# Splitting the opening loads of a fused attention and MLP kernel over two issuing engines, and reordering two later loads

## The chip, the cores and the metric

The kernel runs on one core of one Trainium2 chip. Five engines run their own instruction streams and meet only at semaphores: TensorE (PE, with its weight loads shown apart as PEld), VectorE (DVE), ScalarE (ACT), GpSimd (POOL) and SyncE (SP). SP does no arithmetic here; its queue issues nearly all transfers. The metric is the time of one execution in microseconds of device time. Before the change it is 271.74 us, the median of three runs (271.39 to 272.91).

## The reference

One transformer layer of 2048 tokens and 640 features. The input x is layer-normalised once, and the result feeds two branches whose sum is added to x.

- Attention is a linear attention with 32 heads of 20 features. Queries and keys are each multiplied by a small matrix `w_phi` per head; the feature map is the softmax of that and the softmax of its negative, side by side (40 features). Keys and values are summed over all tokens into a 40 x 20 matrix for each head; queries read from it, divided by a normaliser, and the result goes through `wo`.
- The MLP is a gated one: `silu(xn @ w1) * (xn @ w3)` of 1536 columns, times `w2`.

```
x = A_x
xn = _layernorm(x, axis=-1)
return x + _A_ref(xn, A_wqkv, A_w_phi, A_wo) + _B_ref(xn, B_w1, B_w3, B_w2)
```

All inputs and weights are bfloat16; sums are kept in float32.

## The kernel before

**Tiling.** The 2048 tokens are 16 tiles of 128 tokens (`x_tok`). Each is normalised in place and transposed into `xnT`, which has features on the partitions. Tiles 0 to 3 are transposed by PE and copied out of PSUM; tiles 4 to 15 by transposing transfers from SP's queue. From `xnT` come the values (`wv`), the keys and queries with `w_phi` folded into their weights (`Wkp`, `Wqp`), and the MLP in four blocks of 512 tokens by 12 column chunks of 128. One MLP unit is 10 matmuls of 512 columns, a tanh on ACT and two products on DVE. A fold multiplies a transposed weight (`wqkT`, loaded by a transposing transfer, keys and queries as two halves) by the block-diagonal form of `w_phi` (`BDc`); five folds make `Wkp` and five make `Wqp`.

**What sets the order.** Nothing is scheduled by hand at the level of instructions. A planner written in Python runs when the kernel is built. Fourteen streams (generators such as `norms`, `transposes`, `loads`, `attention`, `mlps`, `queries`) each offer their next step. The planner has an estimated cost for each instruction and a model of the transfers, so it knows for each step when it could start. It takes the one that could start first; among equals, the stream that stands earlier in the list. `attention` (rank 3) thus goes ahead of `mlps` (rank 12) when both could start as soon as PE is free. What the planner chose is fixed in the program: each engine then works through its list in order and waits on semaphores. So a step that is late on the chip holds up everything behind it on the same engine, whatever else could have run.

**Opening.** `first_loads` issues everything the first 20 us need. SP issues half of tile 0, tiles 1 and 2, half of `wv` (its 320 left columns, all five chunks of 128 rows), tile 3, the other half of `wv`, columns 0 to 511 of `w1` and `w3` (`w_s` in the profile), `phi`, the key half of `wqkT` and tiles 4 to 11. ACT issues one transfer, the other half of tile 0; the load of its activation table and a warm-up exponential follow in `consts`. `warm_up` and `idle` give PE matmuls without use before its first data. Tile 1's mean and variance are taken by ACT (`act_sum`), those of the other tiles by DVE; the power of -1/2 is on POOL. In DVE's list the mean of tile 1 (`scalar_op`) stands ahead of the normalising of tile 0, and the variance of tile 1 (in `act_rstd`) ahead of the statistics of tile 2.

**Middle.** When tile 9 has been transposed, `loads` issues, all on SP: columns 512 to 1023 of `w1` and `w3`, tiles 12 to 15, columns 1024 to 1535 of `w1` and `w3`, and the query half of `wqkT`. Then it goes on with the transposes of tiles 10 to 15. `attention` folds one chunk of the query weights behind each of tiles 9 to 13; `mlps` may use a column chunk `fc` only once `done["w"]` exceeds it, and no block of 512 tokens before its four tiles are transposed.

**Normalising.** `ln_apply` gives a tile from 4 on to DVE when DVE is free earlier than ACT by the planner's clocks, and else to ACT. The planner's costs are 0.45 us on DVE and 0.9 us on ACT.

Of the kernel before, what the change touches and what calls it, by code (L numbers as in the profile page):

```python
# [3 lines left out]
ACT = mybir.ActivationFunctionType  # L4
# [5 lines left out]
D = 640  # L10
# [4 lines left out]
DC = D // 128  # L15
# [232 lines left out]
def bass_parallel_sum__linear_kernel_hedgehog__glu_gated_swiglu__prompt_kernel(  # L248
# [16 lines left out]
    P = _Program(nc)  # L265
# [12 lines left out]
    def new(name, shape, dtype, offset=None):  # L278
        size = mybir.dt.size(dtype)
        for n in shape[1:]:  # L280
            size *= n
        return P.sbuf(name, shape, dtype, region(size) if offset is None else offset)
# [22 lines left out]
    x_tok = new("x_tok", [128, T, D], bf, RX)  # L305
# [5 lines left out]
    wv = new("wv", [128, DC, D], bf, RKV + 6400)  # L311
# [86 lines left out]
    x_t = A_x.rearrange("b (t p) d -> p (b t) d", p=128)  # L398
    out_t = out.rearrange("b (t p) d -> p (b t) d", p=128)
    wqkv_t = A_wqkv.rearrange("(c p) n -> p c n", p=128)  # L400
# [4 lines left out]
    def w13(a, b):  # L405
        P.dma("SP", w1_s[:, :, a:b], w1_t[:, :, a:b])
        P.dma("SP", w3_s[:, :, a:b], w3_t[:, :, a:b])

    def load_x(a, b):
        P.dma("SP", x_tok[:, a:b, :], x_t[:, a:b, :])  # L410

    def first_loads():
        def part_wv(a, b):
            P.dma("SP", wv[:, :, a:b], wqkv_t[:, :, 2 * D + a:2 * D + b])

        P.dma("SP", x_tok[:, 0, 0:320], x_t[:, 0, 0:320])
        P.dma("ACT", x_tok[:, 0, 320:D], x_t[:, 0, 320:D])
        load_x(1, 2)
        load_x(2, 3)
        part_wv(0, 320)  # L420
        load_x(3, 4)
        part_wv(320, D)
        w13(0, 512)
        P.dma("SP", phi_s[:], phi_t)
        P.dma("SP", wqkT[:, DC:2 * DC, :], A_wqkv[:, D:2 * D], True)
        load_x(4, 8)
        load_x(8, 12)
# [63 lines left out]

    def ln_apply(t):
        o, m, s, z = x_tok[:, t, :], mv[:, t, 0:1], rstd[:, t, 0:1], rstd[:, t, 1:2]
        if t < 4 or P.free["DVE"] < P.free["ACT"]:
            P.op("DVE", "tensor_scalar", [o], [o, m, s],
                 (o, o, m, s, ALU.add if t == 1 else ALU.subtract, ALU.mult),
                 cost=0.45)
        else:
            P.op("ACT", "activation", [o], [o, s, z], (o, o, ACT.Identity), dict(bias=z, scale=s),
                 cost=0.9)  # L500
# [225 lines left out]
    done = dict.fromkeys(("w", "ln", "t", "f", "k", "n", "kv", "v", "u", "qp", "qn", "qd", "q", "o", "h"), 0)  # L726

    def norms():
        yield lambda: (first_loads(), consts())
        yield lambda: act_sum(1, ACT.Copy, bst[:, 1, 0:1])  # L730
        yield lambda: (ln_half(0, 0), ln_half(0, 1), ln_rstd(0, 1))
        yield lambda: scalar_op(1, mv[:, 1, 0:1], bst[:, 1, 0:1], -1.0 / D, 0.0)
        yield lambda: act_sum(1, ACT.Square, mv[:, 1, 1:2], mv[:, 1, 0:1])
        yield lambda: ln_apply(0)
        done["ln"] = 1
        yield lambda: act_rstd(1)
        yield lambda: ln_half(2, 0)
        while done["t"] < 1:
            yield None
        yield lambda: ln_apply(1)  # L740
        done["ln"] = 2
        yield lambda: ln_half(2, 1)
        yield lambda: ln_rstd(2, 1)
        yield lambda: ln_half(3, 0)
        yield lambda: ln_apply(2)
        done["ln"] = 3
        yield lambda: (ln_half(3, 1), ln_rstd(3, 1))
# [48 lines left out]
    def loads():  # L796
        while done["t"] < 4:
            yield None
        for t in range(4, T):
            while done["ln"] <= t:  # L800
                yield None
            yield lambda t=t: P.dma("SP", xnT[:, :, t * 128:(t + 1) * 128], x_tok[:, t, :], True)
            done["t"] = t + 1
            if t == 9:
                yield lambda: (w13(512, 1024), load_x(12, 16))
                done["w"] = 8
                yield lambda: w13(1024, 1536)
                done["w"] = 12
                yield lambda: P.dma("SP", wqkT[:, 0:DC, :], A_wqkv[:, 0:D], True)
                done["f"] = 2  # L810

    def attention():
        def v(t):
            return lambda: v_tile(t, banks(2))

        yield warm_up
        for t in range(4):
            while done["t"] <= t:
                yield None
            k = banks(2)  # L820
            held.add(k // 2)
            for q in range(2):
                for i in range(DC):
                    yield lambda t=t, q=q, i=i, k=k: v_part(t, q, i, k)
            yield lambda t=t, k=k: v_store(t, k)
            held.clear()
        while done["f"] < 1:
            yield None
        for t in range(T):
            while done["t"] <= t:  # L830
                yield None
            yield lambda t=t: k_tile(t, banks(2))
            done["k"] = t + 1
            if t >= 4:
                yield v(t)
            if 9 <= t < 14:
                while done["f"] < 2:
                    yield None
                yield lambda dc=t - 9: fold_mm(0, dc, banks(2))
        yield lambda: P.dma("SP", wo_s[:], A_wo.rearrange("(c p) d -> p c d", p=128))  # L840
        done["v"] = 1
# [70 lines left out]
    def outs():  # L912
        for t in range(T):
            while done["o"] <= t or done["h"] <= t // 4:
# [4 lines left out]
    URGENT = {0: 4.0, 4: 4.0}  # L919
    PROMPT = (6, 8, 10, 11)  # L920
    streams = [norms(), transposes(), fold_k(), attention(), k_norms(), loads(), key_values(),
               q_toks(), q_norms(), queries(), q_transposes(), o_transposes(), mlps(), outs()]
    n = len(streams)
# [100 lines left out]
```

## Time and profile before

| | us |
|---|---|
| median of three runs | 271.74 (271.39 to 272.91) |
| the profiled execution | 271.42 |
| its span, first to last instruction | 269.7 |
| PE busy | 264.3 (98%) |
| DVE busy | 170.9 (63%) |
| ACT busy | 102.5 (38%) |
| POOL busy | 98.7 (37%) |
| granted clock of PE | 1.00 |

All instructions are issued from one helper line, so they are told apart by tile and operation. The name ahead of the arrow is the tile written, those behind it are read: `PS<-wv,xnT` is a value projection into PSUM, `PS<-xnT,w_s` an MLP matmul, `PS<-BDc,wqkT` a fold, `PS<-ident,x_tok` a transpose on PE. A trailing bracket gives the idle time of the engine before the instruction and what ended it. SPq and ACTq are issues of transfers by SP and ACT; a queue's issue time is not the transfer's. Matmuls overlap one another, so that the distance of their starts, and not the length of one, is what they cost.

### The profile page before, as it was taken

To read this page: it belongs to the slowest core of one execution; us is meant where nothing else is said; L and a number is where in the kernel's file an instruction comes from. 1 tells how busy PE (TensorE), PEld (TensorE's weight loads), DVE (VectorE), ACT (ScalarE), POOL (GpSimd) and SP (SyncE) were. 2 spreads that over 40 slices of the span, in tenths; PEclk is the share of its full clock that TensorE was granted. 3 is DMA by queue.
4 is the path that set the end of the run, shared out by engine and by line. 5 is a ranking of instruction groups with operands and counts; after the bars stand their busy time and mean duration, and the time that the engine had idled before them with its cause. 6 is when DMAs were issued, how large, how long until landed. Compare 5 with 4: busy or idle time off the path is not lost.

```text
span 269.7 us, 4850 instructions
## 1 busy us (share of the span) xinstructions
PE 264.3 (98%) x1978; PEld 161.4 (60%) x1978; DVE 170.9 (63%) x304; ACT 102.5 (38%) x197; POOL 98.7 (37%) x127
## 2 busy tenths in 40 slices
PE   7899999999999999999999999999999999999996
PEld 4556677567855545445445445455677777777774
DVE  4449899999727977778877779877553331212112
ACT  5547989798364343433243433344300000000000
POOL 4315849899974432244421344412440100000000
PEclk9999999999999999999999999999999999999999
DMA  7980589951093124443124442136336533231201
GB/s 197 297 241 1 114 194 346 175 131 71 2 314 82 34 44 80 79 78 68 33 57 80 78 78 53 33 75 80 78 74 155 108 97 92 75 97 49 90 34 49
DMA packets 63510, 27.73 MB, mean 103 GB/s; under 512 B 49792, under 2 KB 63488, under 8 KB 63488
## 3 DMA queue, kind: packets, MB, share of 16 engines
q1 hardware_dynamic: 63344, 27.35, 43.1%
q8 instruction: 15, 0.25, 0.4%
q10 hardware_dynamic: 144, 0.08, 0.1%
q14 instruction: 7, 0.06, 0.1%
HBM read 12.81 MB, written 2.62 MB: 57 GB/s over the span
## 4 chain that ended last, share of the span: by engine, by line
PE 94%; ACT 2%; DMA 2%; SPq 1%; issue 0%; DVE 0%
PE PS L102 94%; DMA wv<-in_A_wqkv_dram 2%; ACT x_tok L102 1%; SPq L114 1%; ACT xnT L102 1%; ACT th L102 0%; ACT Wqp L102 0%; DVE xres L102 0%
## 5 line engine op out<-in xcount | busy, mean ns | idle before, releaser
L102 PE MATMUL PS<-xnT,w_s 128*128 128x512 bf16 x480 | 108.8, 379 | 0.0
L102 PEld LDWEIGHTS PS<-xnT,w_s 128*128 128x128 bf16 x480 | 45.2, 98 | 49.5 <-ACT Wkp L102 0.2
L102 POOL TENSOR_TENSOR eq<-eq,rq 128x600 bf16<-128x600 bf16 (+1 forms) x32 | 22.7, 730 | 88.6 <-DVE rq L102 88.6
L102 PE MATMUL PS<-w_s,hT 128*128 128x320 bf16 (+2 forms) x384 | 54.9, 299 | 0.0
L102 DVE SCALAR_TENSOR_TENSOR t<-th,PS 128x512 bf16<-128x512 f32 x48 | 32.5, 678 | 31.6 <-ACT th L102 31.6
L102 DVE TENSOR_TENSOR xres<-PS,xres 128x640 bf16<-128x640 f32 (+2 forms) x17 | 13.4, 786 | 54.7 <-PE PS L102 54.7
L102 ACT ACTIVATE th<-PS 128x512 f32<-128x512 f32 x48 | 28.8, 600 | 49.0 <-PE PS L102 49.0
L102 PEld LDWEIGHTS PS<-w_s,hT 128*128 128x128 bf16 x384 | 37.6, 98 | 14.6
L102 POOL TENSOR_TENSOR ekt<-ekt,rS 128x640 bf16<-128x640 bf16 x32 | 39.6, 1272 | 1.8 <-DVE rS L102 1.8
L102 ACT ACTIVATE eq<-PS 128x600 bf16<-128x600 f32 (+1 forms) x72 | 24.8, 412 | 29.8 <-PE PS L102 29.6
L102 DVE SCALAR_TENSOR_TENSOR hT<-t,PS 128x512 bf16<-128x512 bf16 x48 | 33.0, 687 | 1.7
L102 PE MATMUL PS<-wv,xnT 128*128 128x320 bf16 x160 | 24.9, 299 | 1.0 <-DMA wv<-in_A_wqkv_dram 0.6
L102 PE MATMUL PS<-wo_s,oT 128*128 128x320 bf16 (+2 forms) x160 | 24.5, 299 | 0.0
L102 PE MATMUL PS<-Wqp,xnT 128*128 128x512 bf16 (+1 forms) x160 | 24.2, 299 | 0.0
L102 PE MATMUL PS<-Wkp,xnT 128*128 128x320 bf16 x160 | 23.9, 299 | 0.0
L102 ACT ACTIVATE ekt<-PS 128x640 bf16<-128x640 f32 x32 | 22.3, 704 | 3.9 <-PE PS L102 3.4
L102 DVE TENSOR_REDUCE S<-ekt 128x64 f32<-128x1280 bf16 x16 | 23.0, 1439 | 0.0
L102 PEld LDWEIGHTS PS<-Wqp,xnT 128*128 128x128 bf16 x160 | 13.5, 98 | 12.8
L102 POOL TENSOR_TENSOR half<-eq 128x660 f32<-128x660 bf16 x15 | 20.4, 1359 | 0.0
L102 PEld LDWEIGHTS PS<-wv,xnT 128*128 128x128 bf16 x160 | 15.2, 98 | 7.8 <-ACT xnT L102 1.2
L102 PEld LDWEIGHTS PS<-Wkp,xnT 128*128 128x128 bf16 x160 | 15.5, 98 | 6.0
L102 PEld LDWEIGHTS PS<-wo_s,oT 128*128 128x128 bf16 x160 | 15.4, 98 | 5.8
(55 smaller groups left out, 172.5 us busy)
## 6 DMA issues: line engine op xcount, KB each, us to landing
w_s<-in_B_w_dram SPq DMA_DIRECT2D x6, 640.0 KB, 7.3
xres<-in_A_x_dram SPq DMA_DIRECT2D x16, 160.0 KB, 2.7
out_dram<-xres SPq DMA_DIRECT2D x15, 160.0 KB, 1.8
x_tok<-in_A_x_dram SPq DMA_DIRECT2D x3, 640.0 KB, 6.4
w_s<-in_B_w_dram SPq DMA_DIRECT2D x1, 1920.0 KB, 8.7
wv<-in_A_wqkv_dram SPq DMA_DIRECT2D x2, 400.0 KB, 4.7
wo_s<-in_A_wo_dram SPq DMA_DIRECT2D x1, 800.0 KB, 4.8
x_tok<-in_A_x_dram SPq DMA_DIRECT2D x3, 160.0 KB, 3.2
```

What stands on the lines that cost most here:

```text
L102: o = _Op(eng, lambda: m(*args, **kw), r, w, cost)
L114: o = _Op(eng, lambda: m(out, in_), self.regions(in_), self.regions(out), nbytes, True)
```

## The change

Three edits. In `first_loads`, tile 2, tile 3 and chunks 3 and 4 of both halves of `wv` are issued by ACT and no longer by SP; a half of `wv` is now two transfers of three and two chunks. In `loads`, the query half of `wqkT` moves ahead of columns 1024 to 1535 of `w1` and `w3`, which move behind the transposes of all tiles (out of the loop). In `ln_apply`, a tile goes to DVE also where DVE becomes free up to 0.45 us later than ACT, so that the engine that would be done first by the planner's costs takes it.

```diff
     def first_loads():
-        def part_wv(a, b):
-            P.dma("SP", wv[:, :, a:b], wqkv_t[:, :, 2 * D + a:2 * D + b])
+        def part_wv(eng, a, c0, c1):
+            P.dma(eng, wv[:, c0:c1, a:a + 320], wqkv_t[:, c0:c1, 2 * D + a:2 * D + a + 320])
 
         P.dma("SP", x_tok[:, 0, 0:320], x_t[:, 0, 0:320])
         P.dma("ACT", x_tok[:, 0, 320:D], x_t[:, 0, 320:D])
-        load_x(1, 2)
-        load_x(2, 3)
-        part_wv(0, 320)
-        load_x(3, 4)
-        part_wv(320, D)
+        P.dma("SP", x_tok[:, 1, :], x_t[:, 1, :])
+        P.dma("ACT", x_tok[:, 2, :], x_t[:, 2, :])
+        part_wv("SP", 0, 0, 3)
+        part_wv("ACT", 0, 3, DC)
+        P.dma("ACT", x_tok[:, 3, :], x_t[:, 3, :])
+        part_wv("SP", 320, 0, 3)
+        part_wv("ACT", 320, 3, DC)
         w13(0, 512)
...
     def ln_apply(t):
...
-        if t < 4 or P.free["DVE"] < P.free["ACT"]:
+        if t < 4 or P.free["DVE"] < P.free["ACT"] + 0.45:
...
                 yield lambda: (w13(512, 1024), load_x(12, 16))
                 done["w"] = 8
-                yield lambda: w13(1024, 1536)
-                done["w"] = 12
                 yield lambda: P.dma("SP", wqkT[:, 0:DC, :], A_wqkv[:, 0:D], True)
                 done["f"] = 2
+        yield lambda: w13(1024, 1536)
+        done["w"] = 12
```

## The prediction

> **What bounds the kernel now.** I first read the busy time by stage, cut at 13.13, 46.75 and 70 us. The columns are stretch, its length, then busy time and instructions of PE, PEld, DVE, ACT and POOL, the granted clock, the DMA share and GB/s.
>
> ```profile
> 0.00:13.13 13.13, 10.67 (x76) 6.41 (x77) 6.16 (x21) 7.29 (x13) 4.48 (x16) 1.00 0.94 246
> 13.13:46.75 33.62, 33.61 (x241) 22.14 (x242) 28.19 (x52) 26.69 (x41) 20.28 (x34) 1.00 0.66 180
> 46.75:70.00 23.25, 22.84 (x188) 15.67 (x186) 22.77 (x30) 19.73 (x31) 22.41 (x25) 1.00 0.56 114
> 70.00:269.70 199.70, 197.17 (x1482) 117.19 (x1478) 113.79 (x203) 48.75 (x115) 51.55 (x55) 1.00 0.35 79
> ```
>
> TensorE is the bound. It idles 13.13 - 10.67 = 2.46 us in the opening, 0.01 us up to 46.75, 23.25 - 22.84 = 0.41 us up to 70, and 2.53 us afterwards, most of that behind the last matmul. The change removes no matmul, so all it can win lies in the opening and in the 0.41 us. The chain of waits, in order of time (start, length, what), names both places:
>
> ```profile
> 3.22 5.20 DMA wv<-in_A_wqkv_dram
> ...
> 50.78 3.25 ACT x_tok L102 x4
> 54.03 0.59 ACT Wqp L102
> ```
>
> The second half of wv is issued at 3.22 and lands at 8.42. Later four tiles normalised on ACT (3.25 us) stand ahead of the evacuation of a folded query weight, and PE waits for that evacuation. These are the targets of the first and third parts of the edit.
>
> **Part 1, the opening loads.** The same bytes are loaded. Moved to ACT's queue are tile 2, tile 3 and chunks 3 and 4 of both halves of wv. SP loses two issues (eight to six ahead of phi). ACT goes from one issue to five, and everything behind them on ACT waits. The timeline of ACT, and of SP's queue, in the opening (start, length, engine, operation, idle time before and its releaser):
>
> ```profile
> 0.78 0.40 ACTq L114 DMA_DIRECT2D x_tok<-in_A_x_dram  x1
> 1.22 1.28 ACT L102 ACT_TABLE_LOAD   x1 [1.22 <-PEq L1009]
> 2.51 0.21 ACT L102 ACTIVATE warm<-warm 128x8 f32<-128x8 f32 x1
> 3.64 0.74 ACT L102 ACTIVATE t<-x_tok 128x640 bf16<-128x640 bf16 x1 [0.92 <-DMA x_tok<-in_A_x_dram]
> ```
>
> ```profile
> 0.79 1.34 SPq L114 DMA_DIRECT2D x_tok<-in_A_x_dram  x3
> 2.17 0.43 SPq L114 DMA_DIRECT2D wv<-in_A_wqkv_dram  x1
> 2.65 0.53 SPq L114 DMA_DIRECT2D x_tok<-in_A_x_dram  x1
> 3.22 0.43 SPq L114 DMA_DIRECT2D wv<-in_A_wqkv_dram  x1
> 3.69 1.49 SPq L114 DMA_DIRECT2D w_s<-in_B_w_dram  x2
> ```
>
> On ACT the table load starts 0.04 us behind the issue, the warm-up activation ends at 2.72, and the sum over tile 1 starts at 3.64 because the tile has landed only then: 0.92 us of slack. SP's first five issues, of the kinds ACT gets, run from 0.79 to 2.65 + 0.53 = 3.18, or 0.45 each at the rate of the first three. So ACT's five end at about 3.1 instead of 1.18, which is 1.92 later; less the slack, the sum over tile 1 and its square start 1.92 - 0.92 = 1.0 us later.
>
> That delay is on the order of DVE. Its queue has the mean of tile 1 ahead of the normalising of tile 0, and the variance of tile 1 ahead of the statistics of tiles 2 and 3, and DVE takes them in that order. Hence all of DVE's normalising from tile 1 on slides by 1.0 us. The opening on DVE, then on PE:
>
> ```profile
> 6.48 0.45 DVE L102 TENSOR_SCALAR x_tok<-x_tok,mv,rstd 128x640 bf16<-128x640 bf16 x1
> ...
> 8.42 0.45 DVE L102 TENSOR_SCALAR x_tok<-x_tok,mv,rstd 128x640 bf16<-128x640 bf16 x1 [0.26 <-POOL rstd L102]
> ...
> 10.37 0.45 DVE L102 TENSOR_SCALAR x_tok<-x_tok,mv,rstd 128x640 bf16<-128x640 bf16 x1 [0.67 <-POOL rstd L102]
> ```
>
> ```profile
> 7.10 0.44 PE L102 MATMUL PS<-ident,x_tok 128*128 128x128 bf16 x5
> 7.38 0.43 PE L102 MATMUL PS<-wv,xnT 128*128 128x320 bf16 x2
> 8.46 1.53 PE L102 MATMUL PS<-wv,xnT 128*128 128x320 bf16 x10 [0.64 <-DMA wv<-in_A_wqkv_dram]
> 9.83 0.44 PE L102 MATMUL PS<-ident,x_tok 128*128 128x128 bf16 x5
> ...
> 11.89 0.44 PE L102 MATMUL PS<-ident,x_tok 128*128 128x128 bf16 x5
> ```
>
> Tile 1 will be normalised at 6.48 + 0.45 + 1.0 = 7.93 and its transposes start at about 8.0; with them (7.38 - 7.10 = 0.28) and the two matmuls behind them (0.27, since ten take 9.83 - 8.46 = 1.37), the second half of tile 0 starts at about 8.55. Now it starts at 8.46, waiting for wv. The wait of 0.64 us for wv goes, and tile 1 is late in its place. Tile 2 is ready at 8.42 + 0.45 + 1.0 + 0.05 = 9.92, and PE takes it at 9.83 now. Tile 3 is ready at 10.37 + 0.45 + 1.05 = 11.87 against 11.89. So everything slides by about **0.1 us**, where wv alone would have won 0.64.
>
> Neither end is certain. ACT shows one issue, none in a row. If issues cost it no time of the activations at all, the 0.64 us come free; tile 2 (ready at 8.92) and tile 3 (10.87) would allow that. If each issue took the 0.75 us of the w_s row (1.49 / 2), ACT would be done at 0.78 + 5 x 0.75 = 4.53, another 1.4 us later, all of it on PE. I take +0.1, since the 0.40 us of ACT's own row is nearest, and keep -0.64 to +1.5. SP's earlier issue of w_s, phi and the transposed key weights by two issues (0.9 us) is worth nothing, because PE reaches the first of them only after the last projection of tile 3, which starts past 13 us. Were that cover gone, the 0.9 us would be the price or the gain.
>
> The Trainium skill, page "DMA: Bandwidth & Descriptors", section "Issuing engines are not separate DMA queues", speaks against this part: all issuers share the same 16 DMA engines, and a second issuer saves only issue time. By it wv would land earlier by no more than the issue time saved, from 3.22 to about 2.65, or 0.6 us. The trace so far cannot contradict it, having one early issue on ACT. The sum above stands either way, since it doesn't let wv end last.
>
> **Part 2, wq ahead of MLP columns 1024-1535.** SP's queue now, and PE at the places it concerns:
>
> ```profile
> 37.24 2.16 SPq L114 DMA_DIRECT2D w_s<-in_B_w_dram  x2
> 39.45 8.96 SPq L114 DMA_TRANSPOSE wqkT<-in_A_wqkv_dram  x1
> 48.45 2.60 SPq L114 DMA_TRANSPOSE xnT<-x_tok  x2
> ```
>
> ```profile
> 46.75 4.48 PE L102 MATMUL PS<-xnT,w_s 128*128 128x512 bf16 x20
> ...
> 81.99 2.32 PE L102 MATMUL PS<-xnT,w_s 128*128 128x512 bf16 x10
> ```
>
> The landing times of the two wqkT transfers (minimum, median, maximum of issue to landing), then the page's DMA issues (KB each, median us to landing):
>
> ```profile
> DMA to landing us min/median/max: 8.8/10.0/11.2
> ```
>
> ```profile
> w_s<-in_B_w_dram SPq DMA_DIRECT2D x6, 640.0 KB, 7.3
> ...
> xnT<-x_tok SPq DMA_TRANSPOSE x12, 2.7
> ```
>
> The query half of wqkT is issued at 39.45 and lands at 39.45 + 11.2 = 50.6, and the next two tiles' transposes queue behind it until 48.45. PE has nothing of the attention to do from 46.75 and runs two MLP units, 20 matmuls. With two issues less ahead, wqkT starts at 37.24. Its landing: 8.8 us in the opening with about 1.3 MB queued ahead (two w_s of 640 KB), 11.2 us here with 3.2 MB (four w_s and an x_tok of that size); with 1.9 MB ahead (two w_s and x_tok) I estimate 9.6 by proportion, so **46.8**. The fold then precedes the MLP in the planner's order, as its stream has the lower rank at equal start, and PE reaches it at 46.75 + 0.1. It is a near tie, with the bounds 37.24 + 8.8 = 46.0 (no wait) and 37.24 + 11.2 = 48.4 (a wait of 1.6). Tile 10's transpose follows SP's issue, which ends 2.2 us ahead of that landing now (48.41 against 50.6), so it starts at 44.6 and lands at 44.6 + 2.7 = 47.3, while PE wants it at about 47.2. Together I take **+0.15** of new waiting.
>
> MLP columns 1024-1535 go behind the last transposed tile. They will be issued about 57 and land some 7 to 10 us later; the ninth MLP unit, the first to need them, runs at 81.99. Hidden, with 14 us to spare; were PE to want the ninth unit sooner, it would wait for that landing.
>
> **Part 3, the normalising.** The allowance of 0.45 moves tiles for which DVE is behind ACT by less than that: ACT gains 3.25 / 4 = 0.8 us a tile, DVE loses 0.45. What is certain to gain is bounded by PE's idle time, 0.41 us: the four tiles on ACT ahead of the query weight. What speaks against is DVE's 22.77 busy of 23.25 us in that stage, with POOL at 22.41 behind it: each moved tile delays k norms and MLP products by 0.45, and four of them 1.8 us, which reaches PE only if it runs out of other units. With the earlier fold the pile-up ahead of the evacuation no longer forms, so I take -0.4 for parts 2 and 3 together, before the +0.15.
>
> **Sum.** +0.1 - 0.4 + 0.15 = about -0.15 us on the profiled execution, whose 271.42 us (269.7 of span and 1.7 around it) are 0.3 below the median 271.74. On the median: 271.6.
>
> **Rivals.**
> 1. *It works as meant*: the table load isn't held up, wv's 0.64 us and the 0.41 us both go: -1.05, so 270.7. For it: the chain names both waits. Against: ACT's table load began only when its one issue was over. It would need ACT's issues to end by 2.1 (0.92 of slack beyond 1.18) to be whole.
> 2. *PE waits for the query weights* at the fold it now runs ahead of the MLP: SP's issue takes the same 8.96 us and the landing 11.2, so 48.4. Price 48.4 - 46.85 = 1.55, and tile 10 another 0.4 behind it, less the 0.41: +1.6 with the opening, so 273.3. It decides from a landing of 47.2 on. For it: the only transfer at this place took 11.2 us. Against: 3.2 MB were ahead of it then, and 1.9 will be.
> 3. *ACT's issues are slow* (0.75 us each, two engines making descriptors at once): +1.5 - 0.25 = +1.25, so 273.0. From 3.0 on, each 0.1 us later at the end of ACT's issues costs 0.1. Against: ACT's and SP's first issues overlap and take 0.40 and about 0.42.
>
> **Chances.** The forecast of no change 0.60, rival 1 0.16, rival 2 0.15, rival 3 0.09. A measurement of this kernel tells about 0.5%, here 1.36 us, from no change. Rival 1 at 270.7 is past it (270.4) for about a third: with a little from the forecast's edge, 0.07 faster. Rivals 2 and 3 lie around the bound at 273.1, two thirds and half past it, with a little of the forecast's: 0.18 slower. The rest, 0.75, is no change. The range goes from the faster rival less a little, 270.5, to the slower rivals, 273.2; the forecast's own range is 270.9 to 272.4.
>
> **What would show it.** In the profile after: the table load on ACT at about 3.1; tile 1's sum at 4.6; tile 1's transposes at 8.0 and no wait for wv on PE, with one for x_tok instead; tile 3's transposes at 11.9 to 12.0; the query wqkT issued near 37.2 and landing at 46.8; the fold on PE at 46.9 and no MLP pair ahead of it; PE idle in 46.75 to 70 below 0.4. The prediction is wrong if PE is at tile 3 before 11.5 or after 12.4, or if the fold starts after 47.5, or if the order on PE after 14 us has been rearranged so that it waits somewhere later.

## The result and the profile after

The changed kernel takes 275.0 us, the median of six runs (274.08 to 275.63). Its ratio to the kernel before is 1.011, with a 95% interval of 1.0084 to 1.0137. It is slower by 1.1%, and outside the range of the prediction. The profiled execution took 274.08 us, the fastest of the six, with a span of 272.3. So the profile has 2.6 us of span to explain, and the median is another 0.9 us above it.

The busy time by stage, cut as for the kernel before:

```profile
0.00:13.13 13.13, 10.53 (x75) 6.16 (x76) 6.16 (x21) 6.39 (x12) 4.11 (x15) 1.00 0.93 237
13.13:46.75 33.62, 33.36 (x240) 21.75 (x238) 27.54 (x50) 26.03 (x40) 19.96 (x35) 1.00 0.71 162
46.75:70.00 23.25, 22.38 (x177) 15.44 (x175) 21.61 (x29) 18.79 (x30) 20.33 (x23) 1.00 0.54 145
70.00:272.30 202.30, 198.65 (x1496) 117.94 (x1493) 123.08 (x209) 48.95 (x115) 52.98 (x56) 1.00 0.35 78
```

TensorE's idle time grew in the third stage (23.25 - 22.38 = 0.87 us, from 0.41), and in the last one, where the prediction placed nothing (202.30 - 198.65 = 3.65, from 2.53). The chain of waits names the places:

```profile
2.76 6.73 DMA wv<-in_A_wqkv_dram
...
46.11 2.69 DMA xnT<-x_tok
...
84.86 1.71 ACT eq L102 x6
...
86.60 0.69 DVE t L102
...
87.34 182.49 PE PS L102 x1256
```

The last piece starts at 87.34 and has no wait in it: after that PE only works off its list. So all that was lost was lost before 87.34. What PE waited for between 14 and 100 us (in total, times, longest):

```profile
PE PS L102 <- DVE t L102: 1.2, 1, 1.2
PE PS L102 <- DMA wqkT<-in_A_wqkv_dram: 0.6, 1, 0.6
PE PS L102 <- ACT xnT L102: 0.3, 1, 0.3
PE PS L102 <- DMA xnT<-x_tok: 0.2, 1, 0.2
```

Three of the four are new; the 0.3 us for `xnT` of ACT is the copy of tile 3's transposes and was there before. The old wait for `Wqp` near 54 us is gone. Now PE itself, in the opening and from 46 us on:

```profile
7.99 0.45 PE L102 MATMUL PS<-ident,x_tok 128*128 128x128 bf16 x5 [0.36 <-DVE x_tok L102]
8.28 0.95 PE L102 MATMUL PS<-wv,xnT 128*128 128x320 bf16 x5
9.54 1.12 PE L102 MATMUL PS<-wv,xnT 128*128 128x320 bf16 x7 [0.30 <-DMA wv<-in_A_wqkv_dram]
10.50 0.44 PE L102 MATMUL PS<-ident,x_tok 128*128 128x128 bf16 x5
```

```profile
46.06 1.52 PE L102 MATMUL PS<-wv,xnT 128*128 128x320 bf16 x10
48.22 0.48 PE L102 MATMUL PS<-BDc,wqkT 128*128 128x140 bf16 x6 [0.64 <-DMA wqkT<-in_A_wqkv_dram]
48.93 1.52 PE L102 MATMUL PS<-Wkp,xnT 128*128 128x320 bf16 x10 [0.23 <-DMA xnT<-x_tok]
...
68.67 2.88 PE L102 MATMUL PS<-Wqp,xnT 128*128 128x512 bf16 x20
71.39 4.24 PE L102 MATMUL PS<-v,ekt 128*128 128x63 bf16 x132
...
87.34 2.33 PE L102 MATMUL PS<-xnT,w_s 128*128 128x512 bf16 x10 [1.16 <-DVE t L102]
```

A bracket counts idle time only. The prices below go from start to start, against the same group where nothing waits, and are a little higher:

- **Opening, +0.67 us.** Tile 2's transposes start at 10.50 instead of 9.83, behind the late end of `wv`.
- **Middle, +0.63 us.** Ten value matmuls take 1.36 us, so the fold could start at 47.42; it starts at 48.22, which is 0.80 late. Tile 10's keys behind it wait another 0.40. The wait near 54 us, 0.57 from start to start, is gone: 0.80 + 0.40 - 0.57.
- **At 86 to 87 us, +1.32 us.** An MLP unit waits for a product on DVE.

That makes 2.62, all of the 2.6 us. The third place is the largest, and what stands there is an order that the planner chose anew. After, the query projections (`Wqp`) stand at 68.67 ahead of the key-value sums (`PS<-v,ekt`) at 71.39. Before, it was the other way round:

```profile
69.52 4.23 PE L102 MATMUL PS<-v,ekt 128*128 128x63 bf16 x132
73.60 2.88 PE L102 MATMUL PS<-Wqp,xnT 128*128 128x512 bf16 x20
```

The earlier queries (`q` in the names below) hand DVE their sums earlier, while POOL is still at the products of the k norms (the scaling of the keys' softmax, `ekt<-ekt,rS`). DVE of the kernel after, then POOL:

```profile
77.41 0.35 DVE L102 RECIPROCAL rq<-Sq 128x32 f32<-128x32 f32 x1
77.79 4.20 DVE L102 TENSOR_TENSOR rq<-rq,Sq 128x32 f32<-128x32 f32 x1
81.92 0.67 DVE L102 SCALAR_TENSOR_TENSOR t<-th,PS 128x512 bf16<-128x512 f32 x1
```

```profile
59.81 22.13 POOL L102 TENSOR_TENSOR ekt<-ekt,rS 128x640 bf16<-128x640 bf16 x18
82.07 1.42 POOL L102 TENSOR_TENSOR eq<-eq,rq 128x600 bf16<-128x600 bf16 x2
```

A product of 32 columns takes 4.20 us and ends when POOL's stream ends (59.81 + 22.13 = 81.94). The MLP's product `t` behind it on DVE starts at 81.92 and not near 78, and five microseconds later PE waits for one like it.

### The profile page after: what moved, and what is told of

It is laid out like the page before. It is cut to its first block, busy times and chain, and to the rows that moved or that the text cites. A ratio compares the mean times of both kernels' runs of the same rounds, so it can differ in the third digit from the quotient of the medians.

```text
span 272.3 us, 4849 instructions
## 1 busy us (share of the span) xinstructions
PE 264.9 (97%) x1978; PEld 161.3 (59%) x1978; DVE 178.4 (66%) x307; ACT 100.2 (37%) x194; POOL 97.4 (36%) x126
## 3 DMA queue, kind: packets, MB, share of 16 engines
HBM read 12.81 MB, written 2.62 MB: 57 GB/s over the span
## 4 chain that ended last, share of the span: by engine, by line
PE 93%; DMA 3%; ACT 1%; ACTq 1%; DVE 0%; issue 0%
PE PS L102 93%; DMA wv<-in_A_wqkv_dram 2%; DMA xnT<-x_tok 1%; ACT eq L102 1%; ACTq L114 1%; ACT xnT L102 1%; DVE t L102 0%; DVE xres L102 0%
## 5 line engine op out<-in xcount | busy, mean ns | idle before, releaser
L102 POOL TENSOR_TENSOR half<-eq 128x660 f32<-128x660 bf16 x14 | 19.0, 1358 | 0.0
```

Of the source, the lines that this page charges most:

```text
L102: o = _Op(eng, lambda: m(*args, **kw), r, w, cost)
```

## The experiments

All twelve kernels compute the whole reference. Ratios are to the kernel before.

**Each edit alone.** `open_only` has the edit of `first_loads` alone, `order_only` that of `loads` alone, `norm_only` the allowance of 0.45 alone.

> The kernel before with the split opening loads alone; every engine's order of arithmetic is that of the kernel before. If the three losses of the changed kernel are separate, PE starts tile 3's values at 13.8 as in the changed kernel (13.13 before), PE waits no longer than before anywhere after 20 us, and the time is 0.7 us above the kernel before (ratio 1.002 to 1.003). If the later losses grow out of the opening's delay, the waits near 47 and 86 us show here too and the time is 2 us or more above.

Measured: 272.07 us, ratio 1.0017 (1.0003 to 1.0032). No wait is added anywhere later. The last half of `wv` is late, more so than in the profile after. Its row on PE:

```profile
9.98 1.12 PE L102 MATMUL PS<-wv,xnT 128*128 128x320 bf16 x7 [0.85 <-DMA wv<-in_A_wqkv_dram]
```

The opening costs 0.17% by itself, some 0.5 us.

> The kernel before with the transposed wq ahead of MLP columns 1024-1535 alone. If the wait at the fold belongs to this part, PE waits about 1.2 us between 46.5 and 48.5 and not at 54 (0.6 before): 0.6 us above the kernel before. The wait at 86 us should be absent, since the order on PE from 68 us on is that of the kernel before. If that wait belongs to this part as well, 1.9 us above.

Measured: 272.38 us, ratio 1.0027 (1.0011 to 1.0042). `wqkT` was issued at 37.61 and landed at 47.18. On PE:

```profile
45.74 1.52 PE L102 MATMUL PS<-wv,xnT 128*128 128x320 bf16 x10
47.31 0.47 PE L102 MATMUL PS<-BDc,wqkT 128*128 128x140 bf16 x6
47.95 1.52 PE L102 MATMUL PS<-Wkp,xnT 128*128 128x320 bf16 x10 [0.17 <-DMA xnT<-x_tok]
...
54.84 2.11 PE L102 MATMUL PS<-xnT,w_s 128*128 128x512 bf16 x9 [0.33 <-ACT Wqp L102]
```

Alone, the move costs 0.27%, some 0.7 us. Ten value matmuls take 1.36 us, so the fold could start at 45.74 + 1.36 = 47.10 and is 0.21 late; tile 10's keys behind it are another 0.32 late. That is less at the fold than the 1.2 us expected, and the old wait is not removed: three normalised tiles still stand on ACT ahead of the evacuation of `Wqp`. There is no wait at 86 us.

> The kernel before with the allowance of 0.45 us alone. The planner now gives tile 11 to DVE. If the wait at 86 us needs the earlier fold as well (queries planned ahead of the key-value sums only with both), it is absent here and the time is within 0.5 us of the kernel before. If this part alone makes it, PE waits 1.3 us near 86 and the time is 1.3 us above.

Measured: 271.68 us, ratio 1.0007 (0.9998 to 1.0017). No difference that can be told; the wait near 54 us stays at 0.4 us, with four tiles on ACT as before.

The three alone come to 0.17 + 0.27 + 0.07 = 0.51%. The change costs 1.1%.

**Each edit left out.**

> The changed kernel with the opening of the kernel before. If the losses are separate, 0.7 us of the 2.7 go: tile 3's values at 13.1, waits near 47 (about 1.2 us) and near 86 (1.3 us), 2.0 us above the kernel before. If the opening's delay is the root of the later ones, they vanish and it is level with the kernel before.

Measured: 274.51 us, ratio 1.0116 (1.0096 to 1.0137). The second and third edits together cost all of it, 3.1 us where 2.0 were expected. The held product is there (at most 4197 ns), PE waits 1.1 us for DVE's `t`, and another 0.65 for `eqT` at 92.30.

> The changed kernel without the allowance in the normalising: opening and load order alone. Order on PE from 68 us on as before. If the wait near 86 comes only of load order and allowance together, it is absent and the two losses add up: 0.45 + 0.7 = 1.2 us above the kernel before (ratio 1.004). If it comes of the late opening and the load order, 2.5 us or more above.

Measured: 273.05 us, ratio 1.0047 (1.0030 to 1.0065), where the single ratios add up to 0.44%. No wait at 86 us.

> The changed kernel without the move of the transposed wq: opening and allowance. If the wait near 86 needs the move, it is absent and the time is 0.45 + 0.2 = 0.65 us above the kernel before (ratio 1.002 to 1.003). If opening and allowance make it together, 2 us or more above.

Measured: 272.24 us, ratio 1.0019 (1.0009 to 1.0030), where the single ratios add up to 0.24%. No wait at 86 us.

So the first edit adds up with either of the others, and the second and third do not add up with each other: 1.16% against 0.27 + 0.07 = 0.34%. The difference, 0.82% or 2.2 us (by the three intervals good to about 0.3%), is their interplay. Only in kernels that have both do the queries go ahead of the sums.

**The order of the queries.** `q_gate` is the changed kernel with one condition more: no query tile is offered before all k norms are planned.

```diff
-        while done["k"] < T or not done["v"]:
+        while done["k"] < T or not done["v"] or done["n"] < T:
```

> The changed kernel with one condition more for the planner: no query tile before all k norms are planned. The two query tiles then stand behind the key-value sums, as in the kernel before. If their place was what cost the wait near 86 (DVE held by POOL's stream), no instruction on DVE takes 4 us, PE waits less than 0.4 us between 80 and 95, and the time falls to 1.0 to 1.5 us above the kernel before. If the place doesn't matter, it stays 2.7 to 3.1 above.

Measured: 272.48 us, ratio 1.0033 (1.0019 to 1.0047). In place of 1.1% that is 0.33%, 0.9 us, a little less than expected. So 0.77% or 2.1 us hang on that order, again to about 0.3%. PE of `q_gate`, and the group of DVE's products (minimum, median, maximum in ns):

```profile
75.98 4.23 PE L102 MATMUL PS<-v,ekt 128*128 128x63 bf16 x132
80.06 2.88 PE L102 MATMUL PS<-Wqp,xnT 128*128 128x512 bf16 x20
```

```profile
L102 DVE TENSOR_TENSOR rq<-rq,Sq x16: 191/193/194, 89.2 to 210.6; 128x32 f32<-128x32 f32 x16
```

The sums are ahead of the queries again, no product lasts above 194 ns, and PE has no wait between 80 and 95 us. The planner moved more than the queries: three MLP units now stand ahead of the sums, from 69.51. But `slow_model` below, which also has all three edits, has its sums at 69.20 and its queries at 73.50, and no wait at 86 us either.

**The held product.** `ratio_moved` is the changed kernel, with tile 0's product alone emitted on POOL. What is planned, and so the order on PE and ACT, stays as it is.

```diff
+        if t == 0:
+            P.pending[-1].alt = lambda: nc.gpsimd.tensor_tensor(r, r, sv[:, :, 0], ALU.mult)
```

> The changed kernel, same order on PE and ACT, with one instruction moved: the product of sums for query tile 0 (128x32), which took 4.2 us on DVE beside POOL's products instead of 0.19, is issued by POOL. If DVE was held there by POOL's stream of products, DVE's MLP products follow 4 us sooner, PE's wait of 1.3 us near 86 goes and the time is 1.3 us below the changed kernel, 1.4 above the kernel before. If the wait comes of the ACT exponentials of the two query tiles (the chain names them), it stays and the time is that of the changed kernel.

Measured: 273.27 us, ratio 1.0066 (1.0041 to 1.0091). DVE, POOL and PE of this kernel:

```profile
77.89 0.63 DVE L103 SCALAR_TENSOR_TENSOR t<-th,PS 128x512 bf16<-128x512 f32 x1
...
82.53 0.68 DVE L103 SCALAR_TENSOR_TENSOR t<-th,PS 128x512 bf16<-128x512 f32 x1
```

```profile
82.12 0.26 POOL L654 TENSOR_TENSOR rq<-rq,Sq 128x32 f32<-128x32 f32 x1
82.46 2.80 POOL L103 TENSOR_TENSOR eq<-eq,rq 128x600 bf16<-128x600 bf16 x4
```

```profile
47.62 0.48 PE L103 MATMUL PS<-BDc,wqkT 128*128 128x140 bf16 x6
...
85.27 2.32 PE L103 MATMUL PS<-xnT,w_s 128*128 128x512 bf16 x10
88.41 0.53 PE L103 MATMUL PS<-KVc,eqT 128*128 128x63 bf16 x12 [0.82 <-DMA eqT<-eq]
```

DVE's first `t` follows at 77.89 instead of 81.92, and the wait for the third is gone: it starts at 82.53 instead of 86.60. So the held product made PE wait. The chain of the profile after names exponentials of ACT (`eq`) ahead of that `t`; here the `t` runs before those exponentials start (83.83), so it doesn't need them.

The ratio falls by 0.44%, some 1.2 us, good to about 0.4% by the two intervals. Not all of that is shown to be the price of the held product. A new wait takes the place of the old one: an MLP unit takes 2.16 us from start to start, so `KVc` could start at 85.27 + 2.16 = 87.43, and it starts 0.98 late, where 1.32 were lost before. Between these two profiles the place gains 0.34 us. The rest of the 1.09 us by which they differ lies in front of it, above all at the fold, which happens not to wait in this one (47.62). In the new wait, POOL scales the queries of tile 0 behind its stream, at 82.46, and their transpose `eqT` lands only at 88.36. In the kernel before they were scaled no earlier (82.51), but PE had one MLP unit more to do first and reached them at 89.82.

**The opening.** Two things could cost time there: ACT is late, or `wv` is late. `act_late` is the kernel before with ACT kept busy by nine small activations.

```diff
+        for _ in range(9):
+            act(warm[:], warm[:], ACT.Copy)
```

> The kernel before with nine further tiny activations (128x8, 0.2 us each) behind the activation table: ACT's first sum starts about as late as in the changed kernel (1 to 1.4 us later than before), with no transfer added or moved. If the delay of ACT alone makes the opening's loss, tile 3's values start at 13.7 to 14.2. If ACT's delay nearly fits into the wait for wv, which lands at 8.4 to 8.8 as before, they start within 0.4 us of the kernel before (13.1 to 13.5 in its profiles), and the rest of the loss belongs to wv's landing.

Measured: 271.75 us, ratio 0.9997 (0.9986 to 1.0008). ACT, then PE:

```profile
4.78 0.72 ACT L102 ACTIVATE t<-x_tok 128x640 bf16<-128x640 bf16 x1
```

```profile
8.10 0.45 PE L102 MATMUL PS<-ident,x_tok 128*128 128x128 bf16 x5 [0.35 <-DVE x_tok L102]
8.38 1.81 PE L102 MATMUL PS<-wv,xnT 128*128 128x320 bf16 x12
```

ACT's sum over tile 1 is later here than after the change (4.78 against 4.67), tile 1 is as late, and it costs nothing: `wv` landed at 8.36, PE went through twelve matmuls without a gap, and tile 3's values started at 13.35 (13.13 to 13.48 in the other profiles with the old opening).

`open_x` is the kernel before with tiles 2 and 3 issued by ACT and both halves of `wv` whole on SP.

```diff
-        load_x(2, 3)
+        P.dma("ACT", x_tok[:, 2, :], x_t[:, 2, :])
         part_wv(0, 320)
-        load_x(3, 4)
+        P.dma("ACT", x_tok[:, 3, :], x_t[:, 3, :])
```

> Tiles 2 and 3 are issued by ACT, and both halves of wv whole by SP, ahead of w_s on the same queue. If the overtaking of ACT's part of wv by SP's w_s is what made wv late, wv now lands by 8.4 or sooner (nothing on SP's queue can overtake it), ACT's three issues cost nearly none of its 0.9 us of slack, and tile 3's values start at 12.6 to 13.1: 0 to 0.5 us below the kernel before. If two queues in themselves move the bytes more slowly, wv lands near 9.5 here too and the time is 0.6 us above.

Measured: 271.49 us, ratio 1.0009 (0.9985 to 1.0032), no difference that can be told. Both halves are issued in turn by SP, the second at 2.18, and land after (minimum, median, maximum):

```profile
DMA to landing us min/median/max: 5.0/5.5/6.0
```

The second lands at 2.18 + 6.0 = 8.2, and PE no longer waits for it. In the profiles that have `wv` split, its last part was issued by ACT at 2.76 and landed between 9.39 and 9.93.

`act_dummy` was meant to give ACT the issues without the data: the kernel before, with four loads of 32-byte rows on ACT.

```diff
+        for j in range(4):
+            P.dma("ACT", hT1[:, j, 0:16], x_t[:, 15, 0:16])
```

> The opening of the kernel before, with four further tiny loads (32 bytes a row, into memory that is needed only much later) issued by ACT ahead of its activation table: ACT is as late as in the changed kernel, while the real loads stay on SP. If ACT's lateness costs the 0.7 us, tile 3's values start at 13.8 here too. If the late landing of wv costs it, wv lands at 8.4 as before, tile 3's values start at 13.15 to 13.3, and the time is 0.1 us above the kernel before.

Measured: 272.06 us, ratio 1.0016 (1.0000 to 1.0032). It separates nothing: ACT's issues came out as wanted (its table load started at 3.23), but `wv`, still whole on SP's queue and issued at 3.22, landed 6.3 us later at 9.5 instead of 8.42. The small loads are all that was added; in the five profiles with the old opening this landing takes 5.1 to 5.5 us.

**The planner's idea of the transfer.** `slow_model` is the changed kernel whose planner takes the big transposing transfer to be slower, so that it puts an MLP unit ahead of the fold.

```diff
-                self.bus = max(self.bus, t + 0.5) + o.cost / (280e3 if o.part else 305e3)
+                self.bus = max(self.bus, t + 0.5) + o.cost / ((190e3 if o.cost > 5e5 and t > 10 else 280e3) if o.part else 305e3)
```

> The changed kernel with the planner told that the transposed query weights land 1.4 us later (190 instead of 280 KB a us for that transfer). It then puts an MLP unit ahead of the fold. If PE's waits near 47 are only the planner's too early landing, they go (below 0.2 us) and with them 1.0 to 1.2 us; the order behind changes too, and whether the wait near 86 stays isn't foreseen: 0.7 to 1.6 us above the kernel before. If something else holds the fold, the wait near 47 stays.

Measured: 273.02 us, ratio 1.0058 (1.0037 to 1.0080). The waits at the fold and at 86 us are gone, and a new one takes their place. PE, and what stood on ACT:

```profile
56.02 1.53 PE L102 MATMUL PS<-wv,xnT 128*128 128x320 bf16 x10 [1.30 <-ACT ekt L102]
```

```profile
51.22 3.43 ACT L102 ACTIVATE x_tok<-x_tok,rstd 128x640 bf16<-128x640 bf16 x4
```

Four normalised tiles pile up on ACT again, this time ahead of `ekt`. Mending one place moved the wait. Of all twelve, none beats the kernel before.

## Why the prediction was wrong

All three signs that the prediction named came: PE is at tile 3 at 12.56, the fold starts at 48.22, and the order behind has been rearranged so that PE waits later.

**Opening: the step on ACT was right, the one on `wv` failed.** The step said ACT's issues would end at 3.1, tile 1's sum slide to 4.6 and its transposes to 8.0. The rows of ACT, and of PE above:

```profile
3.26 1.28 ACT L102 ACT_TABLE_LOAD   x1 [3.26 <-issue]
...
4.67 0.72 ACT L102 ACTIVATE t<-x_tok 128x640 bf16<-128x640 bf16 x1
```

All of it within 0.2 us, and by `act_late` harmless. The sentence that failed is "The wait of 0.64 us for wv goes, and tile 1 is late in its place". The sum "doesn't let wv end last", as if the landing moved with the issue. The last part was issued 0.46 us earlier (2.76 against 3.22) and landed 1.07 later (2.76 + 6.73 = 9.49 against 8.42). In place of +0.1 the opening cost 0.67 in the profile and 0.17% (0.5 us) by `open_only`. ACT's loads have a queue of their own, by their bytes: q10 has 0.74 MB after, when ACT loads 720 KB, and 0.08 before, when it loads half a tile. The rows after (packets, MB, share of the 16 engines):

```profile
q1 hardware_dynamic: 62544, 26.69, 42.2%
q10 hardware_dynamic: 976, 0.74, 0.9%
```

SP issued `w_s`, `phi` and `wqkT` early, which I had priced at nothing because PE needs them late. They were on the other queue and may have gone past the chunks of `wv` that were still waiting on ACT's. In `open_x`, where `wv` is on the same queue as `w_s` and ahead of it, it landed at 8.2. That `w_s` does the overtaking is argued from these landings and was not tried apart.

It can't be all, for the part of the second half that SP issued itself, at 2.2 and ahead of `w_s` on the same queue, was late as well in four of the seven profiles with the split (8.6 to 9.6; 7.6 to 8.1 in the others). The landings of SP's part and of ACT's after, then the chain of `ratio_moved`, where PE's wait ends with SP's part:

```profile
DMA to landing us min/median/max: 6.4/6.6/6.7
```

```profile
2.17 7.12 DMA wv<-in_A_wqkv_dram
```

SP's part landed at 8.6 after and at 9.3 there, later than the whole half before (8.42), which was issued 1.0 us later. That two queues with loads slow each other, whichever holds the part, is a rival that stays open; `act_dummy` speaks for it. What the runs do show is that the last of `wv` lands later when it is split.

The Trainium skill, page "DMA: Bandwidth & Descriptors", section "Queues, rings and completion order", says that each DMA engine takes turns between the queues it has work for, packet by packet. That both parts landed late agrees with it. From the section quoted in the prediction, the landing was taken to come up to 0.6 us earlier; the trace has it 1.07 later.

**The fold: right in kind, too small.** I named the landing as a near tie at 46.8, with 48.4 as the far bound and rival 2 for it. SP's rows after:

```profile
37.56 8.50 SPq L114 DMA_TRANSPOSE wqkT<-in_A_wqkv_dram  x1
46.11 2.60 SPq L114 DMA_TRANSPOSE xnT<-x_tok  x2
```

The issue was 0.32 later than I took and the landing 10.5 us behind it, at 48.1, not 9.6. In place of "+0.15 of new waiting" stand 0.80 and 0.40. Over the profiles with the move, issue to landing was 9.0 (`no_norm`) to 10.5 us, so 9.6 was a fair middle of a wide spread. At that 9.6, in `order_only`, fold and tile 10 together still waited 0.21 + 0.32 = 0.53 us. So rival 2 came true in part and gives most of the 0.27%. That the move would do no harm to MLP columns 1024-1535 was right: they were issued at 58.0 and 58.6 and landed at most 5.7 us later.

**The gain of 0.4 for parts 2 and 3: came, and was outweighed.** In the profile after, two tiles and not four are normalised on ACT at that place, and the wait near 54 us is gone. Neither edit alone brings that.

**The step that decided: "reaches PE only if it runs out of other units".** This sentence of part 3 puts the delay on DVE at nothing. I counted four tiles of 0.45 us against DVE's slack and left the order of the work as it stood. The order was the thing that changed. With both edits the planner put the queries ahead of the sums, DVE's product met POOL's stream, and PE did run out of units, at 86 us. I had listed a rearranged order only as something that would make the prediction wrong, without a price or a chance. By `no_open` and the singles its price is 2.2 us, by `q_gate` 2.1: more than the 0.51% (1.4 us) of the three edits alone. In the profiles it shows as two waits of PE that take each other's place: for `t` behind the held product, and for `eqT` behind POOL's stream. PE idles 1.16 for `t` in the kernel after, 1.10 and 0.65 for `t` and `eqT` in `no_open`, 0.82 for `eqT` alone in `ratio_moved`, and for neither in `q_gate`. How the 2.2 us divide between the two is not settled. Why the planner needs both edits to choose that order was not taken apart; I only know that neither alone leads to it.

The 0.45 us for a tile on DVE was too small as well. Two of the moved tiles took 1.34 each, while POOL worked at products of the k norms (52.53 to 55.11):

```profile
52.61 2.68 DVE L102 TENSOR_SCALAR x_tok<-x_tok,mv,rstd 128x640 bf16<-128x640 bf16 x2 [1.26 <-POOL rstd L102]
```

Whether that added to the loss was not tried.

Rival 3 (ACT's issues slow) had the place right and the mechanism wrong: issues took 0.39 to 0.53 us, and even the late ACT of `act_late` costs nothing.

## What to carry to other kernels

Where a planner fixes the order, an edit to a load or a cost is also an edit to the order everywhere behind it: compare the order on the busiest engine first, and give "it rearranges" a price and a chance of its own. A second issuing engine brings a second queue, and a load that is issued earlier on it can land later: here 0.46 us and 1.07. The one opening that had `wv` earlier kept it whole, on the queue that holds its competitors, and in front of them; that moved the landing and not measurably the time. Two edits that cost little alone can cost far more together, so leave each one out as well as trying each by itself.

## What the runs showed of the hardware

A DVE product of two SBUF inputs, 0.19 us elsewhere, was held 4.20 us beside POOL products of 22.13 / 18 = 1.23 us each. It started at 77.79 and ended with POOL's stream at 81.94, through parts of four of them. The Trainium skill, page "SBUF — State Buffer", section "Who interferes with whom", says that a DVE instruction with two SBUF inputs contends with a GpSimd instruction that reads SBUF. The trace agrees that they contend; that the wait lasts over several instructions of a stream is more than the page says.

Four loads of 128 rows of 32 bytes, put on another queue, went with a later landing of a 400 KB load: 6.3 us behind its issue in the one profile of `act_dummy`, against 5.1 to 5.5 in five profiles without them.
